# Column products of a spectral layer as pairs of 64-row matmuls, with the rows of x on other partitions

## The chip, the cores and the metric

The kernel runs on one core of a Trainium2 chip. The metric is the device time of one execution in microseconds (us), lower is better; for the kernel before, the median of three runs is given. A core has TensorE (matmuls), VectorE, ScalarE, GpSimd, and SyncE, which here issues nearly all DMA transfers. TensorE writes its results to PSUM, eight banks of 2 KiB per partition; VectorE and ScalarE copy them to SBUF ("eviction").

## The reference

```python
x = A_x                                   # (1, 2048, 640) bf16
xn = _layernorm(x, axis=-1)
# A: a spectral filter
X = rfft2(xn.astype(float32), axes=(-2, -1)) * (w_r + 1j * w_i)   # w: (2048, 321)
A = irfft2(X, s=(2048, 640), axes=(-2, -1)).astype(bfloat16)
# B: a gated unit without an activation
g = einsum("bsd,df->bsf", xn, w_gate)     # w_gate, w_up: (640, 1536)
u = einsum("bsd,df->bsf", xn, w_up)
B = einsum("bsf,fd->bsd", g * u, w_down)  # w_down: (1536, 640)
return x + A + B
```

## The kernel before

All work is cut into some 960 tasks, each for one engine. A table written out by hand, `_PLAN`, lists them in order: (task number, engine, first PSUM bank), with engines 0 TensorE, 1 ScalarE, 2 VectorE, 3 GpSimd, 4 SyncE. Each engine carries out its tasks strictly in that order, and waits by semaphore before a task for whatever it depends on. A task that takes a PSUM bank waits for the copy that frees it. So the table sets the order of the matmuls, of the evictions, and of the DMA transfers on SyncE's queue.

*Loading and normalizing.* x has 2048 rows. Partition p holds rows 16p to 16p+15, and "block" j is row 16p+j of every partition, so there are 16 blocks of 128 rows. `ld_x0a` and `ld_x0b` load the two halves of block 0 (one through SyncE's queue, q1, one through ScalarE's, q10), `ld_x1` to `ld_x3` a block each, `ld_x4` four blocks, `ld_x5` the last eight. Gate and up weights come in five pairs of transfers, `ld_gw0` to `ld_gw8`, by two column tiles (the last by four). Statistics are taken on VectorE (`bn`, L754) or ScalarE (`sm` and `sq`, L736 and L745); `mul` (L795) normalizes in place. Blocks 0 to 3 are transposed by TensorE (L814), the others by DMA transposes `xt4` to `xt15` (L802).

*Gated unit.* `GU` multiplies transposed rows with gate and up weights (L973 for blocks 0 to 3, L951, 512 columns a matmul, for the others), `eG` evicts, `H` (L991, L993) takes the product on VectorE.

*Spectral filter.* The transform over 640 columns is split by factors of 5 and 128; `S1` to `S5` (L857 to L892) do the small part on VectorE. The transform over 2048 rows is split as 64 by 32, 32 being the 16 blocks times a parity r: row 32 s + 16 r + j. `R` (L905) is the 64-point transform over s, one task per block, with a table `sm[:, 1, :]`. Because partition p is 2 s + r, that table is 128x128 with zeros wherever the parities differ: each R is five matmuls of 128 columns into two banks, side by side. `eR` evicts 640 elements per partition into U. `D` (L1034, 64 columns a matmul), `C` (L1053), the product with w (`WM`, L1070), `IA` (L1116) and `I` (L1144) follow; D needs all of U, so all sixteen R. `V1` to `V5` end the inverse transform over the columns.

*Output.* For each block, `ACC` (L1221) accumulates the product with w_down, `IV` (L1233) adds the inverse of R with table `sm[:, 2, :]`, `FINA` copies to one of two output buffers on ScalarE, `FIN` (L1260) adds x, loaded again as `ld_xr` into one of four buffers, and `st_out` stores the block.

Copies out of PSUM share one helper, so on the page they are L681 on ScalarE and L682 on VectorE; all transfers share L675.

Of the kernel before, what the change touches and what calls it, by code (L numbers as in the profile page):

```python
# [241 lines left out]
_R = 64  # L242
# [13 lines left out]
def _build_tables():  # L256
# [6 lines left out]
    fw = np.zeros((_R, _RR, 16, _G, 2, _RR), np.float64)  # L263
    bw = np.zeros((16, _G, 2, _RR, _R, _RR), np.float64)
    for tt in range(16):
        for g in range(_G):
            q = tt * _G + g
            ang = two_pi * ((q * s2) % _R) / _R
            for r in range(_RR):
                fw[:, r, tt, g, 0, r] = np.cos(ang)  # L270
                bw[tt, g, 0, r, :, r] = np.cos(ang)
                if q:
                    fw[:, r, tt, g, 1, r] = -np.sin(ang)
                    bw[tt, g, 1, r, :, r] = np.sin(ang)
                else:
                    fw[:, r, tt, g, 1, r] = np.cos(math.pi * s2)
                    bw[tt, g, 1, r, :, r] = np.cos(math.pi * s2)
    sm[:, 1, :] = fw.reshape(128, 128)
# [122 lines left out]
def _d_act(n):  # L401
# [4 lines left out]
    (10, 0, 2), (11, 4, -1), (18, 2, -1), (8, 3, -1), (12, 1, -1), (19, 2, -1), (20, 2, -1), (21, 1, -1), (14, 4, -1),  # L406
    (36, 1, -1), (22, 2, -1), (23, 2, -1), (0, 3, -1), (24, 0, 4), (37, 1, -1), (13, 4, -1), (28, 2, -1), (27, 2, -1),
    (29, 2, -1), (25, 2, -1), (26, 2, -1), (170, 4, -1), (15, 4, -1), (9, 0, 6), (181, 0, 0), (30, 1, -1), (31, 2, -1),
    (38, 1, -1), (39, 2, -1), (32, 2, -1), (33, 0, 2), (40, 2, -1), (41, 0, 6), (34, 2, -1), (35, 2, -1), (169, 4, -1),
    (43, 1, -1), (44, 1, -1), (182, 2, -1), (45, 1, -1), (46, 2, -1), (47, 2, -1), (179, 0, 4), (180, 1, -1), (183, 2, -1),  # L410
    (42, 1, -1), (112, 2, -1), (191, 0, 2), (192, 1, -1), (189, 0, 5), (190, 1, -1), (1, 4, -1), (172, 4, -1), (48, 0, 4),
    (49, 1, -1), (186, 0, 6), (187, 1, -1), (193, 2, -1), (171, 4, -1), (184, 0, 5), (185, 1, -1), (16, 4, -1), (194, 0, 0),
    (195, 1, -1), (62, 1, -1), (113, 2, -1), (63, 1, -1), (196, 0, 1), (197, 1, -1), (206, 0, 5), (188, 2, -1), (174, 4, -1),
    (173, 4, -1), (3, 4, -1), (64, 1, -1), (204, 0, 7), (207, 1, -1), (65, 1, -1), (53, 2, -1), (114, 2, -1), (51, 2, -1),
    (115, 2, -1), (198, 2, -1), (50, 2, -1), (54, 2, -1), (55, 2, -1), (52, 2, -1), (116, 2, -1), (201, 0, 1), (202, 1, -1),
    (66, 1, -1), (17, 4, -1), (2, 4, -1), (176, 4, -1), (175, 4, -1), (67, 2, -1), (205, 1, -1), (56, 1, -1), (57, 2, -1),
    (70, 2, -1), (199, 0, 6), (200, 1, -1), (58, 2, -1), (71, 4, -1), (177, 4, -1), (209, 0, 3), (210, 1, -1), (203, 2, -1),
    (208, 2, -1), (121, 2, -1), (119, 0, 1), (120, 2, -1), (117, 0, 4), (118, 1, -1), (72, 1, -1), (73, 1, -1), (211, 0, 6),
    (212, 1, -1), (74, 1, -1), (122, 2, -1), (59, 4, -1), (214, 0, 3), (215, 1, -1), (216, 0, 7), (221, 0, 6), (222, 1, -1),
    (75, 1, -1), (217, 1, -1), (213, 2, -1), (76, 1, -1), (219, 0, 1), (220, 1, -1), (224, 0, 5), (225, 1, -1), (82, 1, -1),  # L420
    (226, 0, 4), (227, 1, -1), (83, 1, -1), (123, 2, -1), (124, 2, -1), (77, 2, -1), (218, 2, -1), (178, 4, -1), (231, 0, 0),
    (125, 2, -1), (60, 2, -1), (80, 2, -1), (473, 4, -1), (128, 0, 1), (126, 0, 5), (442, 4, -1), (61, 4, -1), (436, 4, -1),
    (437, 4, -1), (223, 2, -1), (440, 4, -1), (127, 1, -1), (232, 1, -1), (84, 1, -1), (68, 2, -1), (69, 4, -1), (78, 2, -1),
    (229, 0, 3), (230, 1, -1), (129, 1, -1), (85, 1, -1), (228, 2, -1), (241, 0, 7), (130, 2, -1), (233, 2, -1), (131, 2, -1),
    (86, 1, -1), (87, 2, -1), (236, 0, 5), (234, 0, 0), (235, 1, -1), (237, 1, -1), (92, 1, -1), (238, 2, -1), (132, 2, -1),
    (242, 1, -1), (244, 0, 1), (245, 1, -1), (93, 1, -1), (246, 0, 6), (239, 0, 5), (240, 1, -1), (243, 2, -1), (247, 1, -1),
    (94, 1, -1), (133, 2, -1), (90, 2, -1), (248, 2, -1), (134, 2, -1), (251, 0, 7), (252, 1, -1), (95, 1, -1), (96, 1, -1),
    (97, 2, -1), (88, 2, -1), (249, 0, 2), (250, 1, -1), (253, 2, -1), (98, 2, -1), (143, 2, -1), (256, 0, 1), (257, 1, -1),
    (254, 0, 7), (255, 1, -1), (102, 1, -1), (258, 2, -1), (79, 4, -1), (467, 4, -1), (91, 4, -1), (466, 4, -1), (472, 4, -1),
    (435, 4, -1), (89, 4, -1), (471, 4, -1), (6, 4, -1), (434, 4, -1), (438, 4, -1), (4, 4, -1), (261, 0, 5), (135, 0, 3),  # L430
    (136, 1, -1), (262, 1, -1), (141, 0, 1), (142, 1, -1), (103, 1, -1), (259, 0, 7), (260, 1, -1), (263, 2, -1), (144, 2, -1),
    (137, 0, 3), (264, 0, 0), (265, 1, -1), (266, 0, 5), (139, 0, 1), (271, 0, 6), (267, 1, -1), (138, 1, -1), (140, 1, -1),
    (104, 1, -1), (105, 1, -1), (268, 2, -1), (145, 2, -1), (274, 0, 7), (269, 0, 3), (275, 1, -1), (270, 1, -1), (106, 1, -1),
    (281, 0, 5), (276, 0, 2), (279, 0, 3), (272, 1, -1), (273, 2, -1), (286, 0, 0), (146, 2, -1), (147, 2, -1), (280, 1, -1),
    (277, 1, -1), (282, 1, -1), (287, 1, -1), (284, 0, 7), (107, 2, -1), (100, 2, -1), (278, 2, -1), (150, 0, 2), (152, 0, 5),
    (289, 0, 0), (285, 1, -1), (151, 1, -1), (108, 2, -1), (110, 2, -1), (429, 4, -1), (109, 4, -1), (441, 4, -1), (469, 4, -1),
    (470, 4, -1), (283, 2, -1), (288, 2, -1), (156, 2, -1), (148, 0, 3), (149, 1, -1), (432, 4, -1), (439, 4, -1), (153, 1, -1),
    (81, 4, -1), (291, 0, 1), (292, 1, -1), (290, 1, -1), (293, 2, -1), (157, 2, -1), (154, 0, 3), (296, 0, 7), (294, 0, 1),
    (295, 1, -1), (297, 1, -1), (298, 2, -1), (158, 2, -1), (159, 2, -1), (306, 0, 2), (307, 1, -1), (155, 1, -1), (304, 0, 1),
    (299, 0, 2), (301, 0, 6), (302, 1, -1), (300, 1, -1), (305, 1, -1), (309, 0, 3), (310, 1, -1), (311, 0, 0), (312, 1, -1),  # L440
    (303, 2, -1), (314, 0, 7), (160, 2, -1), (167, 0, 5), (168, 1, -1), (315, 2, -1), (163, 0, 1), (165, 0, 3), (166, 1, -1),
    (164, 2, -1), (308, 2, -1), (316, 0, 0), (317, 2, -1), (313, 2, -1), (318, 2, -1), (111, 4, -1), (433, 4, -1), (431, 4, -1),
    (99, 4, -1), (161, 0, 2), (5, 4, -1), (498, 4, -1), (503, 4, -1), (101, 4, -1), (497, 4, -1), (504, 4, -1), (499, 4, -1),
    (501, 4, -1), (468, 4, -1), (162, 1, -1), (321, 0, 4), (322, 1, -1), (446, 0, 1), (448, 2, -1), (447, 1, -1), (443, 0, 5),
    (444, 1, -1), (324, 0, 0), (325, 1, -1), (477, 0, 1), (479, 1, -1), (445, 2, -1), (478, 2, -1), (474, 0, 3), (476, 1, -1),
    (475, 1, -1), (449, 0, 5), (450, 2, -1), (326, 0, 7), (327, 1, -1), (451, 0, 1), (452, 2, -1), (453, 2, -1), (457, 3, -1),
    (319, 0, 0), (320, 1, -1), (508, 0, 4), (510, 1, -1), (509, 1, -1), (334, 0, 3), (335, 1, -1), (331, 0, 6), (332, 1, -1),
    (505, 0, 0), (506, 1, -1), (507, 1, -1), (329, 0, 2), (330, 1, -1), (454, 1, -1), (482, 0, 4), (323, 2, -1), (455, 2, -1),
    (483, 2, -1), (339, 0, 3), (480, 0, 0), (481, 2, -1), (341, 0, 7), (342, 1, -1), (535, 4, -1), (502, 4, -1), (532, 4, -1),
    (528, 4, -1), (430, 4, -1), (531, 4, -1), (456, 3, -1), (458, 0, 6), (464, 0, 2), (459, 1, -1), (465, 1, -1), (340, 1, -1),  # L450
    (349, 0, 5), (536, 0, 6), (538, 1, -1), (537, 1, -1), (462, 0, 1), (336, 0, 4), (328, 2, -1), (484, 2, -1), (486, 2, -1),
    (488, 3, -1), (460, 0, 3), (461, 2, -1), (463, 1, -1), (350, 1, -1), (344, 0, 0), (345, 1, -1), (337, 1, -1), (485, 1, -1),
    (500, 4, -1), (513, 0, 1), (514, 2, -1), (511, 0, 5), (512, 2, -1), (351, 0, 7), (352, 1, -1), (567, 0, 3), (569, 1, -1),
    (568, 1, -1), (359, 0, 0), (360, 1, -1), (487, 3, -1), (495, 0, 2), (491, 0, 1), (496, 2, -1), (346, 0, 7), (347, 1, -1),
    (493, 0, 5), (539, 0, 3), (540, 1, -1), (541, 1, -1), (494, 1, -1), (489, 0, 6), (490, 1, -1), (354, 0, 0), (356, 0, 7),
# [889 lines left out]
```

## Time and profile before

| | |
|---|---|
| Median of three runs | 201.56 us (200.73 to 201.60) |
| Profiled execution, its own time | 201.60 us |
| Span of its instructions | 199.9 us |
| Mean granted TensorE clock | 0.991 of full speed |
| Busy: TensorE, weight loads, VectorE, ScalarE | 97%, 62%, 88%, 70% |
| HBM read, written | 18.89 MB, 2.62 MB |
| Chain of waits that ended last | TensorE 74%, VectorE 13%, DMA 8% |
| R: matmuls and weight loads (L905) | 80 each, from 17.9 to 73.3 us |
| D starts; first reload of x for the output; first store | 74.4 us; 136.9 us; 153.4 us |

On the page, "busy" is time in which an engine had an instruction at work; matmuls overlap, so a single one has a longer duration than its share of a sequence. The span is cut into 40 slices of 5 us for the rows of digits. Waits name the instruction that waited, and the one that ended the wait; a DMA's duration "to landing" runs from the start of its issue.

### The profile page before, as it was taken

The numbers are of one execution on the slowest core, as the hardware profiler recorded it, in microseconds if no ns is written. First come the engines' busy times: TensorE is split into PE (matmuls) and PEld (weight loads), VectorE is DVE, ScalarE is ACT, GpSimd is POOL, SyncE is SP. The second block draws the span as 40 slices with busy tenths as digits, with TensorE's granted clock in tenths as the row PEclk, the third lists the DMA queues.
The fourth block names the chain that finished last, engine by engine and source line by source line (L and its number), as shares of the span: only waits on it lengthen the run. The fifth ranks groups of instructions, "written<-read, shape, count | busy, mean of one in ns | idle before, by whom it ended". The sixth has DMA issues, their size and how long they took to land.

```text
span 199.9 us, 4124 instructions
## 1 busy us (share of the span) xinstructions
PE 192.9 (97%) x1591; PEld 123.2 (62%) x1591; DVE 176.0 (88%) x366; ACT 139.1 (70%) x278; POOL 12.9 (6%) x22
## 2 busy tenths in 40 slices
PE   8899949999999999999999999999999999999995
PEld 8898615445455465555565555557777777777674
DVE  3999993999999989998999998994999999999752
ACT  3999965999966569989998999897504542333330
POOL 1000000000000000302303302230000000000000
PEclk9999997999999999999999999999999999999999
DMA  5999975014409825298462452003401231425422
GB/s 151 318 326 355 196 192 113 7 33 99 133 0 210 107 70 135 63 195 214 123 146 71 118 145 69 0 0 74 159 3 33 67 101 44 153 98 166 120 78 66
DMA packets 29666, 23.73 MB, mean 119 GB/s; under 512 B 10448, under 2 KB 27600, under 8 KB 29520
## 3 DMA queue, kind: packets, MB, share of 16 engines
q1 hardware_dynamic: 29504, 23.41, 44.9%
q8 instruction: 12, 0.20, 0.4%
q10 hardware_dynamic: 144, 0.08, 0.1%
q14 instruction: 6, 0.05, 0.1%
HBM read 18.89 MB, written 2.62 MB: 108 GB/s over the span
## 4 chain that ended last, share of the span: by engine, by line
PE 74%; DVE 13%; DMA 8%; SPq 1%; ACT 1%; issue 1%; DVEq 0%
PE ps L951 44%; PE ps L1221 17%; DMA arena<-in_B_w_up_dram 4%; PE ps L1116 3%; PE ps L1034 2%; PE ps L1053 2%; PE ps L905 2%; DMA out_dram<-arena 2%; DMA arena<-in_A_x_dram 2%; PE ps L1144 2%; PE ps L1233 1%; SPq L675 1%; DVE arena L991 1%; DVE arena L1260 1%; DVE arena L857 1%
## 5 line engine op out<-in xcount | busy, mean ns | idle before, releaser
L681 ACT ACTIVATE arena<-ps 128x512 bf16<-128x512 f32 (+6 forms) x213 | 112.6, 578 | 51.9 <-DMA out_dram<-arena 13.7
L951 PE MATMUL ps<-arena 128*128 128x512 bf16 x420 | 99.0, 382 | 2.8 <-DMA arena<-in_B_w_up_dram 2.8
L951 PEld LDWEIGHTS ps<-arena 128*128 128x128 bf16 x420 | 39.2, 98 | 44.1 <-DMA arena<-in_B_w_up_dram 3.2
L1221 PE MATMUL ps<-arena 128*128 128x320 bf16 (+2 forms) x396 | 57.3, 295 | 0.2 <-ACT arena L681 0.2
L1221 PEld LDWEIGHTS ps<-arena 128*128 128x128 bf16 x396 | 37.5, 98 | 13.8 <-ACT arena L681 0.5
L1070 DVE TENSOR_TENSOR arena<-ps,arena 128x256 bf16<-128x256 f32 x64 | 22.7, 418 | 2.4 <-PE ps L1053 2.3
L991 DVE TENSOR_TENSOR arena<-arena 128x512 bf16<-128x512 bf16 x42 | 18.1, 432 | 4.8 <-ACT arena L681 3.8
L1100 POOL TENSOR_SCALAR arena<-arena 64x252 bf16<-64x252 bf16 x8 | 8.4, 1044 | 107.9 <-DVE arena L1087 107.7
L973 PE MATMUL ps<-arena 128*128 128x128 bf16 (+1 forms) x160 | 13.9, 246 | 0.8 <-DVE arena L778 0.8
L973 PEld LDWEIGHTS ps<-arena 128*128 128x128 bf16 x160 | 12.2, 98 | 1.9 <-DMA arena<-in_B_w_up_dram 0.9
L682 DVE CAST arena<-ps 128x320 bf16<-128x320 f32 (+4 forms) x14 | 8.9, 647 | 2.0 <-PE ps L1116 0.9
L1260 DVE TENSOR_TENSOR arena<-arena 128x640 bf16<-128x640 bf16 x15 | 7.0, 487 | 3.8 <-ACT arena L681 3.8
L745 ACT ACTIVATE arena<-arena 128x640 bf16<-128x640 bf16 x12 | 10.1, 838 | 0.2
L1116 PEld LDWEIGHTS ps<-arena 128*128 128x128 bf16 x160 | 7.8, 116 | 3.0 <-issue 0.5
L736 ACT ACTIVATE arena<-arena 128x640 bf16<-128x640 bf16 x12 | 8.9, 740 | 0.2
L1116 PE MATMUL ps<-arena 128*128 128x64 bf16 x160 | 8.3, 198 | 0.0
L1233 PE MATMUL ps<-arena 128*128 128x320 bf16 (+2 forms) x33 | 8.1, 295 | 0.0
L1034 PEld LDWEIGHTS ps<-arena 128*128 128x128 bf16 x160 | 6.5, 98 | 2.6 <-ACT arena L681 0.5
L857 DVE TENSOR_TENSOR arena<-arena 128x768 f32<-128x768 bf16 (+1 forms) x10 | 7.9, 793 | 0.0
L905 PEld LDWEIGHTS ps<-arena 128*128 128x128 bf16 x80 | 5.7, 104 | 2.7 <-issue 0.8
L1034 PE MATMUL ps<-arena 128*128 128x64 bf16 (+1 forms) x160 | 7.0, 193 | 0.0
L1073 DVE TENSOR_TENSOR arena<-ps,arena 128x260 bf16<-128x260 f32 x16 | 7.0, 438 | 0.0
(61 smaller groups left out, 185.3 us busy)
## 6 DMA issues: line engine op xcount, KB each, us to landing
arena<-in_A_x_dram SPq DMA_DIRECT2D x19, 160.0 KB, 3.0
arena<-in_A_w_i_dram SPq DMA_DIRECT2D x30, 80.2 KB, 2.4
arena<-in_A_w_r_dram SPq DMA_DIRECT2D x30, 80.2 KB, 2.4
out_dram<-arena SPq DMA_DIRECT2D x15, 160.0 KB, 1.9
arena<-in_B_w_up_dram SPq DMA_DIRECT2D x4, 320.0 KB, 5.8
arena<-in_B_w_gate_dram SPq DMA_DIRECT2D x4, 320.0 KB, 6.4
arena<-in_A_x_dram SPq DMA_DIRECT2D x1, 1280.0 KB, 9.5
arena<-c_tf SPq DMA_DIRECT2D x4, 256.0 KB, 3.7
```

The source lines that it names most:

```text
L681: return c.e.activation(dst, src, _ACTF.Copy)
L745: return c.e.activation(v_jk, v_x[:, b, :], _ACTF.Square, scale=-1.0, bias=v_m32[:, b:b + 1], accum_out=v_ss[:, b:b + 1])
L857: c.e.tensor_tensor(uo[:, o, :, 0:3, :], v_xb[:, b:b + nt, 0:6:2, :], v_xb[:, b:b + nt, 5:10:2, :], op)
L905: ins = c.e.matmul(psflat[:, bk * 512 + k * 128: bk * 512 + (k + 1) * 128], st, v_sm[:, 1, :], start=True, stop=True)
L951: ins = c.e.matmul(ps[:, bk, :], v_gw[:, w, j, ft, :], v_xt[:, j, rows], start=(j == 0), stop=(j == 4))
L973: ins = c.e.matmul(ps[:, bk, i * n:(i + 1) * n], v_gw[:, w, j, ft0 + i, :], v_xt[:, j, rows], start=(j == 0), stop=(j == 4))
L991: return c.e.tensor_tensor(v_ht[:, ft0, rows], gb[:, 0, :], gb[:, 1, :], _OP.mult)
L1034: ins = c.e.matmul(ps[:, bk + i, k * 64:k * 64 + n], v_uq[:, k, t + i, :], v_fd[:, k * 128 + w * n: k * 128 + w * n + n], start=True, stop ...
L1070: c.e.tensor_tensor(dst, xh, wv, _OP.mult)
L1116: ins = c.e.matmul(ps[:, bk, 64 * k:64 * k + 64], yl, v_ti[:, q, 0, :], start=True, stop=True)
L1221: ins = c.e.matmul(ps[:, bk, 0:sl3.stop - sl3.start], v_ht[:, ft, a * 128:(a + 1) * 128], v_wd[:, ft, sl3], start=(ft == _FT_ORDER[0]), st ...
L1233: return c.e.matmul(ps[:, bank_of(own), 0:sl3.stop - sl3.start], v_sm[:, 2, :], v_v[:, a, sl3], start=False, stop=True)
```

## The change

1. *Rows on partitions.* Partition p = 64 r + s now holds rows 32 s + 16 r to 32 s + 16 r + 15. All loads of x and all stores of `out` use a DRAM pattern of four dimensions (r, s, block, column) in place of three; bytes and contiguous runs per partition are the same.
2. *R.* The table shrinks to 64 columns, the same for both halves of the partitions. Each of the five matmuls becomes two of 64 rows and 64 columns, one on partitions 0 to 63 into the first bank, one on 64 to 127 into the second. `eR` reads both banks, parity innermost, so that U is laid out as before. The table of IV is permuted alike.
3. *Order.* `_PLAN` is replaced throughout: order, banks, and which of ScalarE and VectorE makes some copies. At the front SyncE's queue is now:

```
before: x0a x2 x1 gw0_1 x3 gw0_0 sm1 gw2_1 gw2_0 x4 gw4_1 gw4_0 tf0 x5 fd gw6_1 gw6_0 xt7 gw8_0 xt4 gw8_1 ...
after:  x0a x2 x1 x3 gw0_0 gw0_1 gw2_1 gw2_0 x4 gw4_1 sm1 gw4_0 x5 gw6_1 gw6_0 gw8_1 gw8_0 xt7 ...
```

The core of the diff, without the tables of numbers:

```diff
-    fw = np.zeros((_R, _RR, 16, _G, 2, _RR), np.float64)
-    bw = np.zeros((16, _G, 2, _RR, _R, _RR), np.float64)
+    fw = np.zeros((_RR, _R, 16, _G, 2), np.float64)
+    bw = np.zeros((16, _G, 2, _RR, _RR, _R), np.float64)
...
-    sm[:, 1, :] = fw.reshape(128, 128)
+    sm[:, 1, 0:64] = fw.reshape(128, 64)
...
+        v_un = V("U").rearrange("p (n a c r) -> p n a c r", a=16, c=2, r=2)
...
-        xv = A_x[0].rearrange("(p j) d -> p j d", j=16)
-        ov = out[0].rearrange("(p j) d -> p j d", j=16)
+        xv = A_x[0].rearrange("(s r j) d -> r s j d", r=2, j=16)
+        ov = out[0].rearrange("(s r j) d -> r s j d", r=2, j=16)
...
-            dma("ld_x%d" % gi, v_x[:, b0:b0 + nb, :], xv[:, b0:b0 + nb, :], ...
+            dma("ld_x%d" % gi, v_x[:, b0:b0 + nb, :], xv[:, :, b0:b0 + nb, :], ...
...
-                        ins = c.e.matmul(psflat[:, bk * 512 + k * 128: bk * 512 + (k + 1) * 128], st, v_sm[:, 1, :],
-                                         start=True, stop=True)
+                        for r in range(2):
+                            ins = c.e.matmul(ps[:, bk + r, 64 * k:64 * k + 64],
+                                             st[64 * r:64 * r + 64], v_sm[64 * r:64 * r + 64, 1, 0:64],
+                                             start=True, stop=True)
                     return ins
-                tr = T("R_%d" % (b + u), "pe", 5 * _d_mm(128), em_r,
+                tr = T("R_%d" % (b + u), "pe", 210.0, em_r,
...
-                    src = psflat[:, bk * 512: bk * 512 + 640].rearrange("p (j q m) -> p j q m", j=5, q=_NQ)
-                    return copy_on(c, v_u[:, :, :, b, :], src)
+                    src = ps[:, bk:bk + 2, 0:320].rearrange("p r (n c) -> p n c r", c=2)
+                    return copy_on(c, v_un[:, :, b], src)
...
-            dma("ld_xr%d" % a, v_xr[:, xs, :], xv[:, a, :], 128 * 1280, [(b_xr, ("r", xs, xs + 1))],
+            dma("ld_xr%d" % a, v_xr[:, xs, :], xv[:, :, a, :], 128 * 1280, [(b_xr, ("r", xs, xs + 1))],
...
-                dma("st_out%d" % a, ov[:, a, :], v_out[:, a % 2], 128 * 1280, [],
+                dma("st_out%d" % a, ov[:, :, a, :], v_out[:, a % 2], 128 * 1280, [],
```

## The prediction

> **What bounds the kernel now.** I read the page first: shares, slices, DMA queues.
>
> ```profile
> PE 192.9 (97%) x1591; PEld 123.2 (62%) x1591; DVE 176.0 (88%) x366; ACT 139.1 (70%) x278; POOL 12.9 (6%) x22
> ...
> PE   8899949999999999999999999999999999999995
> ...
> PEclk9999997999999999999999999999999999999999
> DMA  5999975014409825298462452003401231425422
> GB/s 151 318 326 355 196 192 113 7 33 99 133 0 210 107 70 135 63 195 214 123 146 71 118 145 69 0 0 74 159 3 33 67 101 44 153 98 166 120 78 66
> ...
> q1 hardware_dynamic: 29504, 23.41, 44.9%
> ...
> q10 hardware_dynamic: 144, 0.08, 0.1%
> ```
>
> TensorE is busy nearly throughout; its one dull slice is 25 to 30 us, and the slice after it has a lowered clock. The 16 DMA engines are saturated only in the first 20 us (shares of 9, up to 355 GB/s, about 22 GB/s each). Then the waits:
>
> ```profile
> ACT arena L681 <- DMA out_dram<-arena: 13.7, 8, 3.0
> ...
> PE ps L951 <- DMA arena<-in_B_w_up_dram: 2.8, 1, 2.8
> ```
>
> So the last gate/up load holds TensorE once, for 2.8 us, and stores already hold ScalarE's output copies. The chain of waits around that load shows what the pause does to the clock: five L951 matmuls take 2.18 us where five later ones take 1.08.
>
> ```profile
> 28.95 2.18 PE ps L951 x5
> 31.12 1.07 PE ps L905 x10
> ...
> 45.37 0.56 PE ps L905 x10
> 45.93 1.08 PE ps L951 x5
> ...
> 74.62 0.59 PE ps L1034 x20
> ```
>
> Last, the DMA issues: all x loads and all stores of `out`, the transfers whose DRAM pattern the diff rewrites.
>
> ```profile
> arena<-in_A_x_dram SPq DMA_DIRECT2D x19, 160.0 KB, 3.0
> ...
> out_dram<-arena SPq DMA_DIRECT2D x15, 160.0 KB, 1.9
> ...
> arena<-in_A_x_dram SPq DMA_DIRECT2D x1, 1280.0 KB, 9.5
> ```
>
> **The matmuls.** R now is 16 tasks of five matmuls; ten take 0.56 us at full clock, so one R takes 0.28 us and all take 4.5 us. After, an R is ten matmuls of 64 rows and 64 columns. L1034's 64-column matmuls start 0.59/20 = 29.5 ns apart. If the two halves of a pair run one after the other, R takes 0.295 us (+0.24 us over 16 R); if they fully overlap, 0.148 us (-2.1 us). No row has a 64-row matmul, so I take the middle, -1.1 us. It lies on TensorE's path. The Trainium skill, "TensorEngine Tiling (Array Packing)", section "Tiling Modes", says tiles of different rows run in parallel, but also that changing the tiling mode drains the array; no row here shows either, and by its first half alone the term would be -2.1.
>
> **The eviction and tables.** eR still moves 640 elements per partition in one instruction (703 to 706 ns on ScalarE, 816 on VectorE), but reads two PSUM banks in alternate elements. Its price is between 0 and double: +0.7 us each, 14 on ScalarE, which is 77% busy from 30 to 75 us (34.46 of 45). I take 0, as the 64x642 copies, which also read two banks though one after the other, cost 704 ns. Without that cover it would show as R to D latency, a few us. The tables, U's layout and the row order cost nothing: same sizes, results in the same places.
>
> **The new order.** Per engine the tasks keep nearly their old order; 19 of the copies change between ScalarE and VectorE. On SyncE gw8, the last gate/up pair, now follows gw6 directly; before, gw8 stood behind transposes xt7 and xt4, issued at 18.33 and 20.57 us, which wait for VectorE. The loads that it now passes (tf0, fd) are first read when D starts, at 74.62 us. So the 2.75 us stall goes, and the half-clock stretch behind it (1.10 on L951 and 0.51 on L905, 1.6 us). What is late next is VectorE (9.97 of 10 us busy in 10 to 20 and in 20 to 30), so some of this may come back.
>
> **The DMA patterns.** To put even and odd row blocks on the two partition halves, every x load and every store now has a DRAM pattern led by r (2), then s (64), where it had 128 rows. What such a pattern does is the largest unknown. The rows: queue q10 carries one transfer, `ld_x0b`, of 128 rows, and 144 packets, so 16 closing packets. The trace has 2,512 packets of 4 bytes on q1 and q10, 16 for each of 157 transfers and transposes. So transfers led by 128 rows and weight loads led by 32 rows are both dealt to 16 parts, and both counts divide by 16. None is led by less. Bounds: still 16 parts, 0 us; or dealt by the leading count, so two engines carry all of x and `out`.
>
> The second bound, from packet records (median: 640 bytes 32 ns, 1,280 bytes 55, 5,120 bytes 196, 10,240 bytes 385, 512 bytes 27). On two engines, a transfer of 128 packets puts 64 on each.
> - Front: x0's halves 4.1 us, x1 to x3 10.6, x4 12.5, x5 24.6, and shares of the six gate/up loads queued before x5 (40 x 27 ns each) 6.5 and sm 0.2: 58.5 us. First packet at 1.84 us, so x5 lands at about 60.6 in place of 18.6 (issue 9.10 + 9.5). The first statistics of block 8 (L736 on ScalarE) ran at 19.24, right behind that landing; queued behind it on ScalarE are the evictions that TensorE needs for banks. No work covers this: +42.0.
> - gw8 has its share behind x5 (2 x 1.08 + 2 x 1.84 = 5.8 us), landing at 66.4; its user came 9.7 us after block 8's statistics, at about 68 with the stall gone. The stall stays gone: -2.75. The clock term I drop here, since long idle stretches lower the clock again.
> - Tail: between the first store's issue (153.40) and the end (199.9), 46.5 us, lie 12 x loads and the bytes of 16 stores, 28 x 64 x 55 ns = 98.6 us, plus some 1.9 for a first landing: +54. The four x loads before, 14 us, hide in 136.88 to 153.4. Stores free the two output buffers, so ScalarE's copies, banks and TensorE wait on them.
>
> I take the second bound. The nearest rows show a transfer cut into equal parts of its leading dimension, two rows a part for 32 rows; nothing shows an inner dimension being re-cut.
>
> The Trainium skill speaks against the change here: "DMA: Bandwidth & Descriptors", section "Why a DMA increments its semaphore by 16 and not by 1", says the engine count is the largest one up to 16 that divides both patterns' slowest dimension. By that rule the sum is the second bound's; by the rows' 16 parts it is the first's.
>
> **The sum.** Profiled execution: 201.6 us, span 199.9, 1.7 around it; the median of runs is 201.56, so it is a typical one. 201.6 + 42.0 + 54 - 2.75 - 1.1 = 293.7; I say 293. Its own range is 255 to 322: below, one of front and tail is half hidden (for instance stores dealt in 16, 28 us less); above, packets slow as the trace's slower quarter does (the 5,120-byte packets: 216 ns or more for 196), 10% on the 157 us of queueing, and the clock falls while TensorE starves.
>
> **The rivals.**
> - *Transfers still dealt to 16, so faster.* 201.6 - 2.75 - 1.6 - 1.1 = 196.1, with some lost to VectorE 196.5; 194 to 200. For it: packet count and size per transfer don't change, and 128 pieces are there to deal. Against: every row that shows 16 parts has a leading count that holds 16. It decides if a 160 KB x load still lands in about 3 us.
> - *Dealt to 16, but the new forms cost.* Pairs don't overlap (+0.24) and each eR doubles (0.7 x 14 = 9.9 us on ScalarE, with, say, a third on the path), the stall gain half lost: 201.6 + 0.2 + 3.3 - 2.2 = 203; 201 to 206. Against it: the two-bank copies at 704 ns.
> - *The change doesn't do what it says*: pairs run one by one, and the order gains nothing: 201.6 + 0.24, about 202. Little speaks for it, since the stalling load is issued earlier.
>
> **How the numbers follow.** Two engines: 0.68, of which some 0.60 lies in 255 to 322. Still 16 and faster: 0.23. Still 16, no gain: 0.04 for no change, 0.05 for slower. The predicted time is the first case's, 293. The range must reach to the second case to leave out no more than 2 in 10: 195 to 322. Faster by over 0.5% (what the runs' spread of 200.73 to 201.6 lets one tell) 0.23, within 0.5% 0.04, slower 0.73.
>
> **What would show it.** For two engines: the 1,280 KB load takes over 30 us to land, 160 KB x loads over 4 us; each transfer closes with 2 packets, so q10 falls to 130 and q1 by 40 x 14 to 28,944; slices from 25 us on with low TensorE share, first statistics of block 8 near 61 us; ScalarE's wait for stores far above 13.7 us. For the matmuls: R's ten in 0.15 to 0.30 us. For the order: no wait of L951 on the up load. I am wrong if the packet counts stay at 144 and 29,504: then the time is near 196.

## The result, and the profile after

The kernel after takes 311.94 us (median of four runs, 311.24 to 312.47) against 201.58 for the kernel before on the same chip (200.73 to 202.25): a ratio of 1.548, 95% interval 1.541 to 1.555, slower. Its profiled execution took 311.44 us, its span is 309.7 us, and the mean granted clock of TensorE fell from 0.991 to 0.827. Here and below, a time is the median, and a ratio with its 95% interval the comparison, of a kernel's fast runs alone: those within 1.5% of its fastest. Most lines of the source moved down by one to three: L951 of before is L954 of after, L905 is L907, L736 is L737, L1221 is L1224, the copies are L682 and L683, the transfers L676.

The page of the kernel after, the same rows as shown for before (a slice is now 7.7 us):

```profile
PE 211.4 (68%) x1671; PEld 128.4 (41%) x1671; DVE 176.1 (57%) x365; ACT 138.2 (45%) x279; POOL 13.0 (4%) x22
...
PE   5165390059999999999999966963970693915620
...
PEclk9569576559999999999999995995897598775955
...
GB/s 28 123 159 94 86 56 91 107 138 102 129 101 37 230 158 37 128 105 158 94 107 47 1 96 47 5 39 27 39 48 48 37 41 49 51 39 48 48 45 39
...
q1 hardware_dynamic: 28944, 23.40, 27.6%
...
q10 hardware_dynamic: 130, 0.08, 0.1%
```

Read the two packet counts first. The bytes are the same, but q10's one transfer now closes with 2 packets (128 + 2) where it had 16, and q1 lost 560 = 40 x 14. So every x load and every store is carried by two engines. The packet records agree: while `ld_x5` moves, two of its packets are open at once for 0.91 of the time. The GB/s row shows what that is worth: 27 to 51 in the last 14 slices, where before had 33 to 166 in its last 10 (of 5 us each). TensorE starves at both ends, in the first nine slices and on and off in the last seventeen, and is full in between.

The waits of the kernel after (who waited for whom: us in total, times, longest):

```profile
ACT arena L682 <- DMA out_dram<-arena: 69.1, 10, 14.5
...
ACT arena L737 <- DMA arena<-in_A_x_dram: 32.5, 4, 19.3
...
PE ps L1224 <- DMA arena<-in_B_w_down_dram: 4.9, 1, 4.9
```

ScalarE's wait for stores, 13.7 us before, is 69.1; its statistics wait 32.5 us for x; and the matmuls with w_down wait for a load that held nobody before. The up load no longer appears as what holds L954. The chain of waits (start, length, what):

```profile
27.48 35.63 DMA arena<-in_A_x_dram
...
63.14 0.83 ACT arena L737 x2
...
65.19 6.55 PE ps L954 x20
71.73 0.40 PE ps L907 x20
...
172.21 4.32 PE ps L954 x20
...
178.63 9.50 DMA arena<-in_B_w_down_dram
...
188.18 10.19 PE ps L1224 x59
...
201.78 11.96 DMA out_dram<-arena
...
281.27 13.29 DMA out_dram<-arena
```

`ld_x5` is issued at 27.48 and lands at 63.11; block 8's statistics start at 63.14. Cut at the five places that the prediction used (start, block 8's statistics, start of D, first reload of x, first store, end), the kernel after has these windows (length, then busy time of each engine, granted clock, DMA share, GB/s):

```profile
0.00:63.14 63.14, 24.63 (x250) 21.30 (x250) 17.09 (x53) 16.07 (x39) 0.60 (x6) 0.70 0.31 98
63.14:115.40 52.26, 50.21 (x351) 22.55 (x352) 48.13 (x91) 43.42 (x91) 0.00 (x0) 0.94 0.55 122
115.40:177.45 62.05, 61.82 (x572) 34.34 (x569) 57.13 (x130) 56.90 (x104) 12.38 (x16) 1.00 0.34 87
177.45:200.60 23.15, 18.26 (x147) 12.94 (x145) 15.75 (x25) 6.91 (x14) 0.00 (x0) 0.85 0.18 50
200.60:309.70 109.10, 56.47 (x363) 37.24 (x361) 37.97 (x69) 14.90 (x34) 0.00 (x0) 0.74 0.13 43
```

| stage | before | after | added | predicted |
|---|---|---|---|---|
| start to block 8's statistics | 19.24 | 63.14 | +43.9 | +42.0 |
| to D, and to the first reload | 55.2 and 62.45 | 52.3 and 62.05 | -3.3 | -3.85 |
| to the first store | 16.5 | 23.15 | +6.6 | 0 |
| to the end | 46.5 | 109.1 | +62.6 | +54 |
| sum | 199.9 | 309.7 | +109.8 | +92 |

A DMA share of 0.13 in the last window is 2.1 engines of 16: the two that carry x and `out` are nearly always at work, and the others have next to nothing to do.

### The profile page after: what moved, and what is told of

It reads as the page before. It is cut to its first block, busy times and chain, and to the rows that moved or that the text cites. A ratio compares the mean times of both kernels' runs of the same rounds, so it can differ in the third digit from the quotient of the medians.

```text
span 309.7 us, 4277 instructions
## 1 busy us (share of the span) xinstructions
PE 211.4 (68%) x1671; PEld 128.4 (41%) x1671; DVE 176.1 (57%) x365; ACT 138.2 (45%) x279; POOL 13.0 (4%) x22
## 3 DMA queue, kind: packets, MB, share of 16 engines
q1 hardware_dynamic: 28944, 23.40, 27.6%
## 4 chain that ended last, share of the span: by engine, by line
DMA 40%; PE 40%; SPq 11%; DVE 3%; ACT 2%; issue 1%; DVEq 0%
PE ps L954 30%; DMA arena<-in_A_x_dram 20%; DMA out_dram<-arena 17%; SPq L676 11%; PE ps L1224 4%; DMA arena<-in_B_w_down_dram 3%; PE ps L1119 2%; ACT arena L682 2%; DVE arena L1263 2%; PE ps L1037 2%; PE ps L1056 2%; PE ps L907 1%; DVE arena L1180 0%; ACT arena L737 0%; DVE arena L1245 0%
## 5 line engine op out<-in xcount | busy, mean ns | idle before, releaser
L682 ACT ACTIVATE arena<-ps 128x512 bf16<-128x512 f32 (+6 forms) x215 | 112.4, 577 | 117.7 <-DMA out_dram<-arena 69.1
L954 PE MATMUL ps<-arena 128*128 128x512 bf16 x420 | 98.7, 385 | 18.8 <-ACT arena L682 18.8
L1224 PE MATMUL ps<-arena 128*128 128x320 bf16 (+2 forms) x396 | 70.1, 337 | 42.5 <-ACT arena L682 32.3
L1224 PEld LDWEIGHTS ps<-arena 128*128 128x128 bf16 x396 | 42.3, 111 | 64.2 <-ACT arena L682 33.9
L954 PEld LDWEIGHTS ps<-arena 128*128 128x128 bf16 x420 | 39.4, 99 | 62.8 <-issue 21.6
L976 PE MATMUL ps<-arena 128*128 128x128 bf16 (+1 forms) x160 | 17.9, 282 | 16.8 <-DVE arena L880 8.7
L737 ACT ACTIVATE arena<-arena 128x640 bf16<-128x640 bf16 x12 | 8.9, 741 | 32.6 <-DMA arena<-in_A_x_dram 32.5
L976 PEld LDWEIGHTS ps<-arena 128*128 128x128 bf16 x160 | 14.6, 114 | 19.5 <-DMA arena<-in_B_w_gate_dram 17.3
L996 DVE TENSOR_TENSOR arena<-arena 128x256 bf16<-128x256 bf16 (+1 forms) x8 | 2.8, 350 | 22.2 <-ACT arena L682 22.2
L755 DVE BATCH_NORM_STATS2 arena<-arena 128x6 f32<-128x320 bf16 x8 | 3.6, 485 | 20.6 <-DMA arena<-in_A_x_dram 20.6
L683 POOL COPY arena<-arena 64x252 bf16<-64x252 bf16 x8 | 4.4, 546 | 138.8 <-DVE arena L1090 138.5
L683 DVE CAST arena<-ps 128x512 bf16<-128x512 f32 (+4 forms) x12 | 7.8, 673 | 2.4 <-PE ps L954 0.9
L1119 PEld LDWEIGHTS ps<-arena 128*128 128x128 bf16 x160 | 7.7, 117 | 3.4 <-ACT arena L682 0.5
L1236 PE MATMUL ps<-arena 128*128 128x320 bf16 (+2 forms) x33 | 8.4, 298 | 0.0
L1147 PE MATMUL ps<-arena 128*128 128x128 bf16 x80 | 6.7, 225 | 2.3 <-ACT arena L682 2.3
```

The source lines that it names most:

```text
L682: return c.e.activation(dst, src, _ACTF.Copy)
L683: return c.e.tensor_copy(dst, src)
L737: return c.e.activation(v_jk, v_x[:, b, :], _ACTF.Copy, scale=1.0 / _D, accum_out=v_m32[:, b:b + 1])
L954: ins = c.e.matmul(ps[:, bk, :], v_gw[:, w, j, ft, :], v_xt[:, j, rows], start=(j == 0), stop=(j == 4))
L976: ins = c.e.matmul(ps[:, bk, i * n:(i + 1) * n], v_gw[:, w, j, ft0 + i, :], v_xt[:, j, rows], start=(j == 0), stop=(j == 4))
L1119: ins = c.e.matmul(ps[:, bk, 64 * k:64 * k + 64], yl, v_ti[:, q, 0, :], start=True, stop=True)
```

## The experiments

The theory: the leading count of a pattern is the number of engines that carry the transfer, and the time follows from it. The rival: something else in the new loads and stores (their form, the dealt rows), or the new R or the new order, makes them slow.

### Before, with nothing but the rows dealt: led by 2, 4, 8 and 16

Old R (its table's rows permuted alike), old order. Only this differs, with c = 2, 4, 8, 16:

```diff
-        xv = A_x[0].rearrange("(p j) d -> p j d", j=16)
+        xv = A_x[0].rearrange("(t c j) d -> c t j d", c=C, j=16)   # ov alike
```

> The kernel before with one edit: the rows are dealt to the partitions as in the change, so that all x loads and stores have a DRAM pattern led by 2; R stays five full matmuls of 128 columns and the order is the old one. Theory (the leading count is the number of DMA engines): the whole loss is here, 312 to 318 us, 130 packets on q10 and 28,944 on q1. Rival (64-row pairs or the new order cost the time): about 202 us.

> As the run with 2, but the rows are dealt so that the DRAM pattern is led by 4 and has 32 inside. Theory of the engine count: four engines carry x and out; x5 lands near 35.5 us in place of 18.6 (+17), the last part takes about 56 us for 46.5 (+9): 228 us, 220 to 238; q10 132 packets, q1 29,024. Rival (a pattern of this form, with jumps of 20 KB and more between rows and an extra dimension, is slow in itself): as slow as with 2, about 312 us.

> Pattern led by 8, with 16 inside. Theory of the engine count: x5 lands near 22.6 us (+4), the last part's 27 us of transfers hide again: 206 us, 203 to 211; q10 136 packets, q1 29,184. Rival (the form of the pattern is slow): about 312 us.

> Pattern led by 16, with 8 inside: as many dimensions as with 2, and longer jumps between rows. Theory of the engine count: all 16 engines, the time of the kernel before, 201.6 us, 199 to 205; q10 144 packets, q1 29,504. Rival (the form of the pattern is slow): about 312 us.

Measured against 201.62 us for before on that chip. The columns to the right come from the profiles, of one execution each: what each stage adds to before, and the mean time of one 10,240-byte packet of `ld_x5`.

| led by | us | ratio (95%) | q10 packets | to first reload | to first store | to end | x5 packet |
|---|---|---|---|---|---|---|---|
| 2 | 313.93 | 1.560 (1.552 to 1.568) | 130 | +40.0 | +12.6 | +58.4 | 394 ns |
| 4 | 250.68 | 1.247 (1.237 to 1.256) | 132 | +21.1 | +6.0 | +20.8 | 459 ns |
| 8 | 217.15 | 1.080 (1.072 to 1.087) | 136 | +12.2 | +1.4 | +3.2 | 676 ns |
| 16 | 207.26 | 1.029 (1.023 to 1.034) | 144 | +5.9 | +0.4 | +1.0 | 758 ns |
| 128 (before) | 201.62 | 1 | 144 | 0 | 0 | 0 | 388 ns |

Led by 2, before takes what after takes, without its R and its order, as expected: the pattern alone is the slowdown. The packet counts follow the leading count exactly, and so does the number of `ld_x5` packets open at once (two, four and eight for most of the time, led by 2, 4 and 8). The rival that such a pattern is slow in itself expected 312 us also of 4, 8 and 16, and falls. But the expectations for 4, 8 and 16 were too low, by 23, 11 and 6 us, and led by 16 has all 16 engines and still loses 6 us, nearly all of it in the front. The last column shows a second cost that grows while the first shrinks: a packet of the same 10,240 bytes takes 388 ns in before and 758 led by 16.

### After, with each x load and store as two transfers of 64 partitions

```diff
-    ins = c.e.dma_start(dst, src)                      # src[r, s, ...], led by 2
+    for r in range(2):                                 # led by 64
+        ins = c.e.dma_start(dst[64 * r:64 * r + 64], src[r])   # stores alike
```

It was run with after's R and order, with the old R, with the old order, and with both old.

> The changed kernel with one edit: each x load, reload and store is issued as two transfers of 64 partitions, each with a pattern led by 64. Theory of the engine count: both loss terms go, 16 engines carry each half; the stretch between block 8's statistics and the first reload was 3.4 us shorter in the changed kernel than before, and 40 more issues of about 0.43 us on SyncE's queue cost up to 1 us at the front: 198 us, 195 to 201. Rival (the form of the pattern, jumps of 40 KB): about 310 us.

> As the run with halves, but R undone: block-diagonal table, five full matmuls of 128 columns and the old eviction. Theory: an R was 0.20 us in the changed profile and 0.28 before, 16 of them 1.3 us on TensorE's path: 1 us slower than the run with halves, 0 to 2. Rival (the pairs also free the eviction or the following stage): over 2 us slower; or nothing, if VectorE sets the stretch.

> As the run with halves, with the order and banks of the kernel before. Theory: the wait for the last gate/up load (2.75 us) and its half-clock stretch (1.6 us) come back, partly hidden: 2 to 4.5 us slower than the run with halves. Rival (the order only moves waits about): within 1 us.

> As the run with halves, with R and the order of the kernel before: what is left of the change are the rows' places and 40 more issues. Theory: 201.6 us plus 0 to 1.5 us for the issues. Rival (the issues on SyncE's queue delay the loads at the front by 3 us and more): 204 us or over.

Before took 200.16 us on that chip.

| | new order | old order |
|---|---|---|
| new R (pairs) | 213.33, ratio 1.068 (1.060 to 1.076) | 217.06, ratio 1.083 (1.075 to 1.090) |
| old R | 213.65, ratio 1.066 (1.059 to 1.074) | 216.92, ratio 1.084 (1.078 to 1.090) |

Some 97 of after's 110 us come back, again without touching R or the order. The order is worth about 3.5 us (3.7 and 3.3 in the two rows; 2 to 4.5 was expected). The pairs show nothing in the total: +0.3 and -0.1 us for the old R, where the intervals are some 1.6 us to each side. All four miss the expectation of 198 to 203 us by 14 to 17 us, so the second cost is here too, and larger. With both old, the rival that the issues delay the front by 3 us and more (204 us or over) held. In that profile, the stages are 6.7, 2.0 and 6.7 us longer than in before. The tail has a reason that the chain of waits shows: the issues themselves (SPq, SyncE's queue), 26.5% of the chain from the first store on where before has 2.6%:

```profile
190.78 0.49 SPq L684
...
191.31 0.60 SPq L684
...
195.75 2.12 DMA out_dram<-arena
```

Each issue takes 0.60 us where before's plain one takes 0.43, and there are twice as many: from the first store on 60 issues, some 36 us of a stage of 53.2, where before has 30, some 13 us of 46.5. The front has the issues as well (the first 17 transfers of SyncE's queue in before are issued by 12.57 us, led by 16 by 15.13, with the x loads as halves by 17.72), and beside them x5's packets, 741 ns. How much of the front belongs to each was not measured.

### What makes a packet of 10,240 bytes take 388 or 758 ns

A kernel that leaves the computation out and only loads x, in nine ways, each waited for before the next, twice over. `w` is a tile of 128 partitions:

```python
"plain128":  (w, rows p)                 "lead16":    (w, rows dealt, led by 16)
"low64":     (w[0:64],  rows 2 s)        "mid64":     (w[32:96], rows 2 s)
"run_low64": (w[0:64],  rows 0 to 63)    "run_mid64": (w[32:96], rows 0 to 63)
"two_one_queue", "two_two_queues": (w[0:64], rows 2 s), (w[64:128], rows 2 s + 1)
"lead2":     (w, rows dealt, led by 2)
```

> This kernel leaves the whole computation out. It makes nine kinds of load of x, each by itself and waited for, twice over, all with packets of 10,240 B as x5 has: plain128 (before's load, 128 rows to 128 partitions), lead16 (the same rows dealt, pattern led by 16), low64 and mid64 (the same 64 rows, every second one, to partitions 0-63 and to 32-95), run_low64 and run_mid64 (64 neighbouring rows to 0-63 and to 32-95), two_one_queue and two_two_queues (both halves, 0-63 and 64-127, on SyncE's queue, or one on ScalarE's), lead2 (after's load). What is open is why a 10,240 B packet of x5 took 388 ns in before, 758 in lead16 and 741 in halves with the old order and R, all with 16 engines, and 385 in after with two. Theory: the 16 engines meet in pairs on the destination side, which partitions are written at once decides: low64 and run_low64 near 750 ns a packet, mid64 and run_mid64 near 390, plain128 390, lead16 750, lead2 385, two_one_queue 750, two_two_queues 390 to 600. Rival 1, the dealt rows in DRAM: low64 and mid64 both near 750, run_low64 and run_mid64 both near 390. Rival 2, the issue's form (anything but plain 128 rows): all but plain128 and lead2 near 750, wherever they land. By itself: the Trainium skill, page 'SBUF — State Buffer', section 'Door 1: The DMA port swizzle (why [64,N] ≈ [32,N])', has a formula by which partitions 0-63 reach half of 16 ports and 32-95 all of them, which would say what the theory says.

The timeline of SyncE's queue, first pass (start and length of the issue; since each is waited for, the next start tells when it had landed; a tile's trailing number is left out of its name, so the last line is `lead2`):

```profile
0.73 0.39 SPq L44 DMA_DIRECT2D plain<-in_A_x_dram  x1
6.53 0.66 SPq L44 DMA_DIRECT2D lead<-in_A_x_dram  x1
15.12 0.50 SPq L44 DMA_DIRECT2D low<-in_A_x_dram  x1
20.61 0.55 SPq L44 DMA_DIRECT2D mid<-in_A_x_dram  x1
24.91 0.48 SPq L44 DMA_DIRECT2D run_low<-in_A_x_dram  x1
30.56 0.53 SPq L44 DMA_DIRECT2D run_mid<-in_A_x_dram  x1
34.74 1.11 SPq L44 DMA_DIRECT2D two_one_queue<-in_A_x_dram  x2
43.49 0.47 SPq L44 DMA_DIRECT2D two_two_queues<-in_A_x_dram  x1
...
52.14 0.62 SPq L44 DMA_DIRECT2D lead<-in_A_x_dram  x1
```

| | bytes | from issue to the next | packet, mean of pass 1, pass 2 | median, pass 1 |
|---|---|---|---|---|
| plain128 | 1,280 KB | 5.80 us | 454, 461 ns | 385 |
| lead16 | 1,280 KB | 8.59 | 716, 714 | 768 |
| low64 | 640 KB | 5.49 | 712, 747 | 770 |
| mid64 | 640 KB | 4.30 | 541, 500 | 385 |
| run_low64 | 640 KB | 5.65 | 712, 700 | 766 |
| run_mid64 | 640 KB | 4.18 | 549, 525 | 385 |
| two_one_queue | 1,280 KB | 8.75 | 747, 749 | 774 |
| two_two_queues | 1,280 KB | 8.65 | 768, 760 | 771 |
| lead2 | 1,280 KB | 27.11 | 399, 398 | 385 |

`low64` and `mid64` read the same rows with the same form of instruction, and only the partitions differ: 0 to 63, or 32 to 95. To 0 to 63 the median packet takes twice as long (770 against 385 ns). `run_low64` and `run_mid64` say the same with rows that are neighbours, so neither the dealt rows nor the form of the issue is the cause of this doubling; both rivals fall. The means of the middle ones, 500 to 549, were expected near 390; some of their packets are still slow, and the whole transfer is longer by a factor of only 1.3. One part of the theory fell as well: to spread the two halves over two queues changes nothing (8.65 against 8.75 us).

The Trainium skill, "SBUF — State Buffer", section "Door 1: The DMA port swizzle (why `[64,N]` ≈ `[32,N]`)", has a formula by which partitions 0 to 63 reach 8 of 16 ports of the memory and 32 to 95 reach all 16. The measured factor of two in the median packet agrees with it; the whole transfers differ by less. That led by 16 suffers for the same reason, by which partitions its engines write at the same time, is argued from the formula and not shown; no run here shows which engine writes which partition.

### What one transfer costs in a stream

A kernel that leaves the computation out and moves ten blocks of 160 KB back to back, as loads and then as stores, in each way; then ten loads and ten stores led by 2 in turn; last, a long load led by 2 with plain loads issued behind it.

> This kernel leaves the whole computation out. On SyncE's queue it issues ten blocks of x (160 KB each, 1,280 B packets) back to back and waits for all ten, first as loads and then as stores, for each way of moving them: plain (before), led by 16, two halves of 64 partitions, led by 2 (after); then ten loads and ten stores led by 2 in turn, as after's tail has them; and last a load of 1,280 KB led by 2 with six plain loads of 160 KB and two of 320 KB issued behind it. Theory, engine count: from first issue to last landing a set of ten takes 7 us plain (10 x 0.43 us of issue and 2.5 to land), 9 led by 16 (10 x 0.6), 14.5 as halves (20 x 0.6), and 36 to 40 led by 2 (640 packets for each of two engines at 55 to 59 ns, the issues stretched to 3.5 us), loads like stores; the twenty in turn take 72 to 83 us (55 to 64.5 ns, as after's tail: 109.1 us for 27, 4.04 us each). The plain loads behind the long one land only after it, 25 us (64 x 385 ns) from its issue or later. Rival 1 (the two engines were slowed by the kernel's other traffic, not by their number): led by 2 under 25 us. Rival 2 (engines take packets of several transfers in turn, after's w_down load was late for another reason): the plain loads land within 8 us, long before the long one.

The windows of its ten sets (length of each, granted clock, DMA share, GB/s): plain loads, plain stores, led by 16 loads and stores, halves loads and stores, led by 2 loads and stores, led by 2 in turn, the long load with what follows it.

```profile
0.70:8.86 8.16, 0.00 (x0) 1.00 0.67 201
8.86:15.12 6.26, 0.00 (x0) 1.00 0.75 262
15.12:24.11 8.99, 0.00 (x0) 1.00 0.66 182
24.11:32.46 8.35, 0.00 (x0) 1.00 0.64 196
32.46:46.93 14.47, 0.00 (x0) 1.00 0.43 113
46.93:61.37 14.44, 0.00 (x0) 1.00 0.47 114
61.37:97.59 36.22, 0.00 (x0) 1.00 0.13 45
97.59:133.31 35.72, 0.00 (x0) 1.00 0.13 46
133.31:203.81 70.50, 0.00 (x0) 1.00 0.13 46
203.81:237.89 34.08, 0.00 (x0) 1.00 0.29 87
```

With nothing else on the core ten loads take 8.16 us plain, 8.99 led by 16, 14.47 as halves and 36.22 led by 2; ten stores take 6.26, 8.35, 14.44 and 35.72. Those in turn take 70.5 / 20 = 3.53 us each, 55 ns for each of an engine's 64 packets; 72 to 83 us had been expected for the twenty. The rival that the kernel's other traffic slowed the two engines falls. Halves are bound by their issues: 20 in 12.67 of the 14.47 us.

The plain loads behind the long one split. In the packet records, counted from the long load's first packet, 672 of their 768 packets of 1,280 bytes moved within 16 us, beside it; the last 96, the shares of two engines in sixteen, moved at 27 to 30.4 us, as the long load ended (its last packet began at 27.5). So a plain transfer is finished only when two busy engines have reached its share. The issuer is held as well:

```profile
203.81 0.54 SPq L34 DMA_DIRECT2D big<-in_A_x_dram  x1
204.40 15.02 SPq L34 DMA_DIRECT2D late<-in_A_x_dram  x6
```

Six plain issues take 15.0 us, where ten took 4.7 at the start of the same kernel.

## Why the prediction was right, and where its sizes were off

- *Two engines.* Right in every count it named: q10 130, q1 28,944, the 1,280 KB load 35.6 us to land. The rows alone (16 parts everywhere) did not decide between the bounds; what decided was that every one of those rows had a leading count that holds 16. The series 2, 4, 8, 16 agrees with the rule that the prediction quoted from the Trainium skill ("DMA: Bandwidth & Descriptors", section "Why a DMA increments its semaphore by 16 and not by 1"); no run here has a leading count, such as 100, that would test its divisor further. One reading was off: 2,512 closing packets are not 16 for each of 157 transfers and transposes, as the trace of before has 133 transfers and 12 transposes; 16 and 32 would give that number.
- *Front, +42.0 against +43.9.* x5 lands at 63.1 where 60.6 was worked out (58.5 us from 1.84 is 60.3), and block 8's statistics start 0.03 us later. The path was as described: x5, ScalarE's statistics, then TensorE.
- *The order.* The wait on the up load is gone, and the two middle stages gave 3.3 us for the 3.85 of order and R together. The halves runs give the order alone 3.3 to 3.7 us. The clock term was dropped rightly: the slow stretch that the order was to take away came back behind x5's landing (the granted clock of the front is 0.70), on the chain, where 20 matmuls of L954 take 6.55 us, and 4.32 later on.
- *R, -1.1 against some -0.2.* The middle of the prediction's bounds is -0.94, not -1.1. The gain lies between these bounds, but not because the pairs overlap in part: they overlap fully, and the change to pairs and back has a price, which the prediction named and gave no term. The timeline of TensorE in after, then in before:

```profile
99.08 0.47 PE L907 MATMUL ps<-arena 64*128 64x64 bf16 x20
...
100.66 0.32 PE L907 MATMUL ps<-arena 64*128 64x64 bf16 x10
100.92 1.25 PE L954 MATMUL ps<-arena 128*128 128x512 bf16 x5
102.10 0.32 PE L907 MATMUL ps<-arena 64*128 64x64 bf16 x10
```

```profile
58.20 0.72 PE L905 MATMUL ps<-arena 128*128 128x128 bf16 x10
...
59.84 0.44 PE L905 MATMUL ps<-arena 128*128 128x128 bf16 x5
...
61.19 0.44 PE L905 MATMUL ps<-arena 128*128 128x128 bf16 x5
```

Go by the starts. Two R and the five matmuls of L954 behind them take 1.58 us in after, and 1.64 in before. One R and five matmuls take 1.44, and 1.35 in before: with a single R the pairs are slower. In the records a pair's two matmuls start 3 to 4 ns apart and pairs 29 ns apart, so an R by itself takes 0.147 us, the full overlap. But at each of the nine stretches of R in after, some 0.1 us is lost ahead of the first pair and some 0.1 behind the last. That is 9 x 0.21 = 1.9 us of the 16 x 0.13 = 2.1 gained, so the pairs save TensorE some 0.2 us, which fits the halves runs.
- *eR reads two banks at no cost.* 708 ns on ScalarE and 820 on VectorE, for 706 and 816: the value taken, 0, and not double.
- *First reload to first store, 0 against +6.65.* The step "the four x loads before, 14 us, hide in 136.88 to 153.4" failed. The x loads hide, but a w_down load is issued behind two of them, and its shares on the two busy engines queue: it landed 9.5 us after its issue at 178.63, and L1224 waited 4.9 us for it. Some 2 us more are the lowered clock behind that pause (0.85 in this stage): 59 matmuls of L1224 take 10.19 us on the chain, an estimated 8.1 at the rate of five just before it, which took 0.69. Before led by 2, with its four reloads queued alike, has the same wait, 11.2 us, and the last set of the stream kernel shows it by itself. It is the step that the prediction applied to gw8 and forgot here.
- *Tail, +54 against +62.6.* The mechanism holds and the term was mis-sized. 27 transfers of 128 packets and the last block's pieces lie in the stage; the records give 204.5 + 9.5 us, on two engines 107 us of the 109.1. A packet took 59.2 ns in the mean, where the prediction took the median, 55, which the clean stream also gives. The mean of before's tail, 64.5, would have missed as far to the other side (+71).
- *The range.* Its lower example was off, though nothing hung on it: with stores dealt to 16, the 12 x loads are 42.2 us on two engines, less than the 46.5 of the stage, so by the prediction's own terms all of the +54 would go and not 28.
- *The sum.* 293 against 311.9 lies inside the range, and the 18 us that are missing have places: 1.9 in the front, 6.6 ahead of the first store and 8.6 in the tail, with 0.5 in the middle. All four err to the same side, so the total was not right by errors that cancelled.

## What to carry to other kernels

Before a view of a DRAM tensor is split into more dimensions, look at what stands in front: a pattern led by 2 was carried by two engines of 16, and 110 us were lost on a rearrangement that saved TensorE some 0.2. A leading count of 16 or 64 brought all engines back, but no run here is a full cure. Two transfers of 64 partitions still cost 13 us, with x5's packets taking nearly twice as long and with twice the issues; one transfer over all 128 partitions led by 16 still cost 6, with packets as slow. Only the plain pattern of 128 rows had both, all engines and short packets. And where small matmuls are packed in pairs, count the changes to them and back: the pairs paid only where several R stood side by side. Read the closing packets per transfer and the landing time of one large load first; they tell the number of engines before any total does.

What stays open: the new order on before's own rows, and dealt first loads of x (as halves on one queue or on two) beside plain reloads and stores, were not measured; by the halves runs the order alone could be worth some 3.5 us there, an estimate. No kernel here beats the one before.

## What the runs showed that had not been expected

- *The issuer stalls.* In the kernel after, SyncE's issues grow once two engines are behind; the timeline of its queue from x5 on:

```profile
27.48 4.07 SPq L676 DMA_DIRECT2D arena<-in_A_x_dram  x1
31.60 3.10 SPq L676 DMA_DIRECT2D arena<-in_B_w_up_dram  x1
34.74 12.56 SPq L676 DMA_DIRECT2D arena<-in_B_w_gate_dram  x1
47.34 11.66 SPq L676 DMA_DIRECT2D arena<-in_B_w_up_dram  x1
```

A weight load takes 12.6 us to issue where before took 0.4 to 1.7, in a stage in which the DMA engines are busy for 0.31 of the time, and everything behind it on the queue waits. The chain puts 11% of the span down to it.
- *The same bytes, twice the median packet, by partition.* 640 KB to partitions 0 to 63 take 5.5 to 5.7 us, to 32 to 95 take 4.2 to 4.5.
- *The form of an issue has a price.* On an idle queue 0.34 to 0.39 us for a plain transfer of 128 rows, 0.47 to 0.66 for all others.
- *64-row pairs overlap fully, and the change costs.* Ten matmuls take 0.147 us, 14.7 ns each; going to pairs and back takes some 0.2 us a time, so that one R alone is 0.09 us slower than before.
